# Interleaving the second batch's banded groups with buffers of their own, moving sums of v and half of the masks off PE, strided transposes with plain copies

## The chip, the cores and the metric

The kernel runs on one core of one Trainium2 chip. The time is device microseconds of the whole program on that core; the number that counts is the median of the runs. Five engines work side by side, each through its own list of instructions in a fixed order: PE (matrix products and transposes), DVE and POOL (elementwise work and reductions), ACT (elementwise functions, copies, scalings) and SP, which issues the transfers between HBM and the on-chip memory SBUF. PE writes into PSUM, eight banks of 128 partitions by 512 floats; DVE and ACT read PSUM, POOL does not.

## The reference

```python
B, H, S, D = 8, 8, 576, 64          # q, k, v: [B, H, S, D] float32, factor = 4, Sd = 144
def sm_attn(qq, kk, vv):
    s = scale * np.matmul(qq, kk.transpose(0, 1, 3, 2))
    s = s - np.max(s, axis=-1, keepdims=True)
    a = np.exp(s)
    a = a / (np.sum(a, axis=-1, keepdims=True) + 1e-09)
    return np.matmul(a, vv)
q_d = q.reshape(B, H, Sd, factor, D).mean(axis=3)     # k_d, v_d alike
out_up = np.repeat(sm_attn(q_d, k_d, v_d), factor, axis=2)
mask = np.abs(pos[:, None] - pos[None, :]) < factor
scores = np.where(mask, scale * np.matmul(q, k.transpose(0, 1, 3, 2)), -1000000000.0)
...
x = (out_up + out_local).transpose(0, 2, 1, 3).reshape(B * S, H * D)     # 4608 x 512
h = np.maximum(np.maximum(x @ w1, x @ w2), x @ w3)                       # 512 -> 768
return (h @ w_out).astype(np.float32)
```

So x is the sum of two attentions per head: one over the sequence pooled by four (144 rows, repeated four times), one local, in which a token sees itself and three neighbours on either side. On x runs a layer with three input matrices, their elementwise maximum, and one output matrix. The weights come as float64 and are decoded on the chip.

## The kernel before

Tokens of a batch are 128 pooled rows of four tokens (512) and a tail of 16 pooled rows. *Block* j (0 to 7) is the first 512 tokens of batch j; block 8 is the tails of all batches. The heads of a batch go in two *groups* of four: group n = 2j or 2j + 1.

For each block the layer (`mlp_in`, `mlp_out`) is 288 matmuls of 128x512 on PE: every product of float32 values is made as three products of split halves (`xhi` × `whi`, `xhi` × `wlo`, `xlo` × `whi`), 216 into `pm` banks for the three input matrices, and 72 for the output. Nine blocks make 2592. `transposes(j, c)` prepares block j: it adds the pooled attention `od` to the local one, then ACT rounds to `xhi` and DVE (or POOL) takes the rest as `xlo`, four tiles c of each.

The local attention is computed in two ways. Groups 4 to 15 multiply shifted windows of k and v with q and with probabilities on DVE, ACT and POOL (`scores`, `values`; names `prod`, `s`, `pv`). Groups 0 to 3 (`DENSE`) use PE, as a banded product. Their steps, by the letters that the order strings use:

- L, `band_load`: q, k, v from HBM (`q4`, `k4`, `vband` in the buffers `wo`).
- T, `band_transposes`: q and k transposed on PE into PSUM, copied into `homes` (they lie in weight buffers, so they are called `whi` and `wlo` in the trace); pairs of tokens are added on DVE into `hd` and `qkT`, the pooled q and k.
- A and B, `band_scores` for one pair of heads each: for every bank a matmul of `identr` with `maskr` puts the band's mask into PSUM, and four products of q and k are added; DVE takes the maximum (`mxb`) and ACT the exponential with its sum; POOL or ACT scales.
- V and W, `band_values`: probabilities transposed (`ptb`), copied, multiplied with `vband`, and turned into `xb` tiles of tag `x`.
- t, `tail_pooled`: the tail's rows (`traw`, `th`, `tq`). p, `pooled_scores`: scores and softmax over the 144 pooled rows (`pd`, `pdt`, `ptl`, `ptd`, `rd`), transposed on PE.
- v, `band_pooled_values`: sums of four tokens of v, as five matmuls of a constant `sums` with `vband` (four of 256 columns and one of six rows; they show as `sums` in the trace), copied to `vd`.
- o, `pooled_values`: the pooled attention's product with `vd`, scaled by ACT into `od` and, for the tail, `odtail`.

What sets the order: every operation is recorded first (`Recorder.add`), with the engines that may run it, and `place` hands them out one at a time: to the engine that could start earliest, among what is ready there by priority (`prio`, less is sooner; PE's operations get 2000 less) and then by place in the program, with durations from `price`. So an operation that two engines may run goes to where it would end sooner by these prices, and a change of a price moves work. `WINDOW` says how many PSUM tiles ahead in the program may take a free bank. The first block is written out as steps in `ORDER`, groups 0 and 1 interleaved, priority 0; group 2 has priority 200 and group 3 300, each written straight through (L T A B V t p W v o). The weights of the first four sixths come at 150 to 210, the layer at −100. Buffers are rings by tag (`prod`, `pd`, `pt`, `y`, `t`, `hqk`, ...); group 1 has a part of its own in `own1`, which lies in the buffer `prod` that group 4 needs later. One line, 374 in before and 378 in the changed kernel, emits everything, so all rows show this line.

Of the kernel before, what the change touches and what calls it, by code (L numbers as in the profile page):

```python
# [40 lines left out]
PE_MASK = (0, 1, 2, 3)  # L41
# [32 lines left out]
WINDOW = {"pa": 4, "pm": 4}  # L74
# [17 lines left out]
class Recorder:  # L92
# [44 lines left out]
    def add(self, forms):  # L137
# [18 lines left out]
        o.need, o.tiles = set(), []  # L156
# [229 lines left out]
def local_global_attention_maxout_kernel(ctx: ExitStack, tc: tile.TileContext, q, k, v, w1, w2, w3, w_out, ident_d, mask_d, diag_d, band_d, out):  # L386
# [46 lines left out]
    sums = new([P, 96 + P], tag="sums", name="sums")  # L433
# [55 lines left out]
    def load_rest():  # L489
# [4 lines left out]
        sp.dma_start(sums, band_d[:, 2 * (P + 6) :])  # L494
# [45 lines left out]
    def tail_pooled(n):  # L540
# [3 lines left out]
        for g, src in enumerate((q, k, v)):  # L544
            raw = new([N64, FAC * D], tag="traw", name=f"traw_{n}_{g}")
# [11 lines left out]
    def pooled_scores(n, tag="pa"):  # L557
# [23 lines left out]
        pd = own(n, 1).rearrange("p (a b x) -> p a b x", a=2, b=2) if n == 1 else new([P, 2, 2, SD], tag="pd", name=f"pd_{n}")  # L581
# [17 lines left out]
        pt = own(n, 2).rearrange("p (g x) -> p g x", g=HH) if n == 1 else new([P, HH, SD], tag="pt", name=f"pt_{n}")  # L599
        ptt = new([N64, P + N64], tag="hqk", bufs=2, name=f"ptt_{n}") if n == 1 else new([N64, P + N64], tag="ptt", name=f"ptt_{n}")  # L600
# [104 lines left out]
    def band_load(n):  # L705
# [10 lines left out]
        kh = st["kh"] = new([3, HH, D], tag="kd" if n == 1 else "qd", name=f"kh_{n}")  # L716
# [83 lines left out]
    def band_values(n, pr, tag):  # L800
# [7 lines left out]
        for i in range(2):  # L808
# [3 lines left out]
            pt = new([P, FAC, P], tag="t" if n == 1 else "y", bufs=2, name=f"ptb_{n}_{pr}_{i}")  # L812
# [100 lines left out]
    def attention(n):  # L913
# [3 lines left out]
        if n in DENSE:  # L917
            band_load(n)
            band_transposes(n, "pa")
            band_scores(n, 0, "pa")  # L920
            band_scores(n, 1, "pa")
            band_values(n, 0, "pa")
            tail_pooled(n)
            pooled_scores(n)
            band_values(n, 1, "pa")
            band_pooled_values(n)
            pooled_values(n)
            return
# [17 lines left out]

    def first_block():
        open_block(0)
        tags = ("pm", "pa")
        load_constants()  # L950
        for n in range(2):
            band_load(n)
        load_rest()
# [3 lines left out]
        steps = {
            "T": lambda n: band_transposes(n, tags[n]),
            "A": lambda n: band_scores(n, 0, tags[n]),
            "B": lambda n: band_scores(n, 1, tags[n]),  # L960
            "t": tail_pooled,
            "p": lambda n: pooled_scores(n, tags[n]),
            "V": lambda n: band_values(n, 0, tags[n]),
            "W": lambda n: band_values(n, 1, tags[n]),
            "v": lambda n: band_pooled_values(n, tags[n]),
            "o": lambda n: pooled_values(n, tags[n]),
        }
        for step in ORDER.split():
            steps[step[0]](int(step[1]))
# [48 lines left out]
```

## Time and profile before

| | us |
|---|---|
| median of 3 runs | 822.71 |
| lowest and highest | 818.24 and 826.49 |
| profiled execution, its time | 821.14 |
| its span in the profile | 819.4 |
| PE busy | 787.8 (96%) |
| DVE busy | 660.5 (81%) |
| ACT busy | 422.2 (52%) |
| POOL busy | 361.6 (44%) |

The span is what the profile covers; the execution's own time is 1.7 us more. All rows that follow are of this one execution, whose granted clock was 0.975 on the mean. A row of a timeline is start, length, engine, line, operation, output<-inputs by buffer names, shape and count; several like rows in line are put together, and a bracket tells idle time before and who ended it. A window's row has, for each engine, its busy time and number of instructions in that stretch, then the granted clock, the share of the DMA engines' time and GB/s.

### The profile page before, as it was taken

To read this page: it belongs to the slowest core of one execution; us is meant where nothing else is said; L and a number is where in the kernel's file an instruction comes from. 1 tells how busy PE (TensorE), PEld (TensorE's weight loads), DVE (VectorE), ACT (ScalarE), POOL (GpSimd) and SP (SyncE) were. 2 spreads that over 40 slices of the span, in tenths; PEclk is the share of its full clock that TensorE was granted. 3 is DMA by queue.
4 is the path that set the end of the run, shared out by engine and by line. 5 is a ranking of instruction groups with operands and counts; after the bars stand their busy time and mean duration, and the time that the engine had idled before them with its cause. 6 is when DMAs were issued, how large, how long until landed. Compare 5 with 4: busy or idle time off the path is not lost.

```text
span 819.4 us, 12160 instructions
## 1 busy us (share of the span) xinstructions
PE 787.8 (96%) x4064; PEld 609.9 (74%) x4064; DVE 660.5 (81%) x859; ACT 422.2 (52%) x1446; POOL 361.6 (44%) x522
## 2 busy tenths in 40 slices
PE   6879999999999999999899999999899999999997
PEld 4657776777777777777677777778677887888885
DVE  5999668799999999999999999999999962231220
ACT  7867657435583737567274746726483451121111
POOL 0642101136878847697477956768162341000000
PEclk9668999999999999999999999999999999999999
DMA  7754033334323423352234334422242210001002
GB/s 243 186 174 118 10 103 110 110 102 131 108 97 107 125 77 90 102 157 84 84 110 135 110 88 113 143 85 88 77 133 73 79 58 26 1 13 39 1 0 52
DMA packets 63177, 76.72 MB, mean 94 GB/s; under 512 B 21484, under 2 KB 43434, under 8 KB 63114
## 3 DMA queue, kind: packets, MB, share of 16 engines
q1 hardware_dynamic: 63114, 75.94, 30.8%
q8 instruction: 32, 0.52, 0.3%
q14 instruction: 31, 0.25, 0.1%
HBM read 66.49 MB, written 9.44 MB: 93 GB/s over the span
## 4 chain that ended last, share of the span: by engine, by line
PE 64%; DVE 20%; ACT 6%; issue 5%; DMA 2%; POOL 2%; POOLq 0%; SPq 0%; DVEq 0%; ACTq 0%
PE pm L374 52%; PE pa L374 11%; DVE prod L374 4%; DVE s L374 3%; DVE x L374 3%; ACT pv L374 2%; POOL pv L374 2%; DVE wo L374 1%; DMA v<-in_v_dram 1%; ACT wlo L374 1%; DVE y L374 1%; DVE pm L374 1%; DVE t L374 1%; DMA pv<-in_k_dram 1%; DVE xlo_0r L374 1%
## 5 line engine op out<-in xcount | busy, mean ns | idle before, releaser
L374 PE MATMUL pm<-xhi_0r,whi_0r 128*128 128x512 f32 x648 | 258.4, 399 | 0.0
L374 PE MATMUL pm<-xhi_0r,wlo_0r 128*128 128x512 f32 x648 | 258.3, 399 | 0.0
L374 PE MATMUL pm<-xlo_0r,whi_0r 128*128 128x512 f32 x648 | 258.2, 399 | 0.0
L374 POOL TENSOR_TENSOR pv<-v,s 128x256 f32<-128x256 f32 x247 | 177.6, 835 | 93.7 <-DVE s L374 72.1
L374 ACT ACTIVATE pv<-v,s 128x64 f32<-128x64 f32 x580 | 151.7, 412 | 21.8 <-DMA v<-in_v_dram 9.8
L374 PEld LDWEIGHTS pm<-xhi_0r,whi_0r 128*128 128x128 f32 x648 | 122.4, 189 | 28.3 <-issue 0.2
L374 PEld LDWEIGHTS pm<-xlo_0r,whi_0r 128*128 128x128 f32 x648 | 122.2, 189 | 28.1 <-issue 0.4
L374 PEld LDWEIGHTS pm<-xhi_0r,wlo_0r 128*128 128x128 f32 x648 | 122.1, 188 | 27.8
L374 DVE TENSOR_TENSOR prod<-k,q 128x1792 f32<-128x1792 f32 x56 | 119.2, 2128 | 1.1 <-DMA k<-in_k_dram 0.9
L374 DVE TENSOR_REDUCE x<-pv 128x256 f32<-128x1792 f32 x55 | 110.2, 2006 | 7.2 <-POOL pv L374 7.1
L374 DVE TENSOR_REDUCE s<-prod 128x28 f32<-128x1792 f32 x56 | 112.4, 2007 | 0.4
L374 DVE TENSOR_TENSOR t<-pm,t 128x512 f32<-128x512 f32 x54 | 36.9, 683 | 63.9 <-PE pm L374 63.8
L374 PE MATMUL pm<-wo_1r,hh_0r 128*128 128x512 f32 x216 | 85.6, 397 | 0.0
L374 PE MATMUL pm<-wo_1r,hh_1r 128*128 128x512 f32 x216 | 85.4, 399 | 0.0
L374 DVE TENSOR_TENSOR pm<-pm,t 128x512 f32<-128x512 f32 x54 | 37.3, 691 | 25.1 <-PE pm L374 24.9
L374 ACT CAST hh_1r<-pm 128x512 fp32r<-128x512 f32 x30 | 17.6, 588 | 71.3 <-DVE pm L374 71.3
L374 ACT COPY t<-pm 128x512 f32<-128x512 f32 x54 | 31.8, 589 | 40.0 <-PE pm L374 39.9
L374 ACT CAST hh_0r<-pm 128x512 fp32r<-128x512 f32 x24 | 14.1, 588 | 67.8 <-DVE pm L374 67.5
L374 PEld LDWEIGHTS pm<-wo_1r,hh_1r 128*128 128x128 f32 x216 | 41.0, 190 | 10.0 <-issue 0.5
L374 ACT COPY y<-pm 128x512 f32<-128x512 f32 x38 | 22.2, 588 | 49.6 <-PE pm L374 42.3
L374 PE MATMUL pm<-wo_0r,hh_1r 128*128 128x512 f32 x120 | 47.5, 400 | 0.1
L374 PEld LDWEIGHTS pm<-wo_1r,hh_0r 128*128 128x128 f32 x216 | 40.9, 189 | 9.1
(262 smaller groups left out, 1142.6 us busy)
## 6 DMA issues: line engine op xcount, KB each, us to landing
v<-in_v_dram SPq DMA_DIRECT2D x55, 320.0 KB
k<-in_k_dram SPq DMA_DIRECT2D x55, 320.0 KB
out_dram<-y SPq DMA_DIRECT2D x36, 256.0 KB
q<-in_q_dram SPq DMA_DIRECT2D x56, 128.0 KB
hh<-in_moe_w_dram SPq DMA_DIRECT2D x12, 512.0 KB
pv<-in_moe_w_dram SPq DMA_DIRECT2D x6, 512.0 KB
pv<-in_moe_w_out_dram SPq DMA_DIRECT2D x6, 512.0 KB
wo<-in_v_dram SPq DMA_DIRECT2D x12, 128.0 KB
```

What stands on the lines that cost most here:

```text
L374: getattr(self.engines[o.eng], method)(*map(real, args), **{k: real(x) for k, x in kw.items()})
```

## The change

Six edits:

1. Group 3 gets buffers of its own as group 1 has them (`OTHER`): its `qkT`, `pd` and `pt` in `own1`, `kh` in `kd`, `ptt` in `hqk`. Only group 1 keeps its `ptb` in `t` (`TY`).
2. Groups 2 and 3 are written in steps, interleaved (`ORDER2`, `second_block`), both at priority 200.
3. In groups 2 and 3 the mask is added by DVE, from PSUM into SBUF, and the maximum and the exponential read it there; the identity matmuls stay in groups 0 and 1 alone (`PE_MASK`).
4. `band_pooled_values` no longer uses PE: v is loaded again, 128 KB for each head, and halved twice by additions on DVE or POOL. The constant `sums` goes.
5. In groups 0 and 1 the transposes of q and k write PSUM in the tokens' order, every fourth word, and the copies out of PSUM become plain; before, the transposes wrote plainly and the copies were strided on both sides.
6. The order's parameters: `WINDOW` from 4 to 3, POOL's price of `tensor_scalar` from 2.2 to 4.1 ns for each element, `traw` of k and v in groups 0 and 1 in the ring `q`. `GATE` and `behind` have empty values and do nothing.

```diff
+OTHER = (1, 3)
+TY = (1,)
+ORDER2 = "L2 T2 L3 A2 B2 V2 W2 T3 t2 p2 A3 B3 v2 o2 V3 W3 t3 p3 v3 o3"
 ORDER = "T0 T1 A0 A1 B0 V0 B1 V1 t0 p0 t1 p1 W0 W1 v0 o0 v1 o1"
-PE_MASK = (0, 1, 2, 3)
+PE_MASK = (0, 1)
-WINDOW = {"pa": 4, "pm": 4}
+WINDOW = {"pa": 3, "pm": 3}
...
             if method == "tensor_copy":
                 return 180.0 + n, True
+            if method == "tensor_scalar":
+                return 140.0 + 4.1 * n, True
...
         sp.dma_start(diag, diag_d)
-        sp.dma_start(sums, band_d[:, 2 * (P + 6) :])
         sp.dma_start(mask, mask_d.rearrange("m p x -> p m x"))
...
         for g, src in enumerate((q, k, v)):
-            raw = new([N64, FAC * D], tag="traw", name=f"traw_{n}_{g}")
+            raw = new([N64, FAC * D], tag="q", bufs=2, name=f"traw_{n}_{g}") if n < 2 and g else new([N64, FAC * D], tag="traw", name=f"traw_{n}_{g}")
...
-        pd = own(n, 1).rearrange("p (a b x) -> p a b x", a=2, b=2) if n == 1 else new([P, 2, 2, SD], tag="pd", name=f"pd_{n}")
+        pd = own(n, 1).rearrange("p (a b x) -> p a b x", a=2, b=2) if n in OTHER else new([P, 2, 2, SD], tag="pd", name=f"pd_{n}")
...
+                    inorder = ps.rearrange("p (r f) -> p f r", f=FAC)
                     for f in range(FAC):
-                        pe.transpose(ps[:, P * f : P * f + P], byf[:, f], ident)
-                    to, fr = dst.rearrange("p (r f) -> p f r", f=FAC), ps.rearrange("p (f r) -> p f r", f=FAC)
+                        pe.transpose(inorder[:, f], byf[:, f], ident)
+                    to, fr = dst, ps
...
-        banks = {}
+        banks, on_pe = {}, n in PE_MASK
...
-            for i in range(2):
+            for i in range(2) if on_pe else ():
                 pe.matmul(sps[i], identr, rest, start=True, stop=False, skip_group_check=True)
-                banks[tp, i] = sps[i]
...
-                    pe.matmul(sps[i][:, u], qT[pp, t0 : t0 + P], kT[pp, t0 : t0 + P + 6], start=False, stop=u == 1, skip_group_check=True)
+                    pe.matmul(sps[i][:, u], qT[pp, t0 : t0 + P], kT[pp, t0 : t0 + P + 6], start=not on_pe, stop=not on_pe or u == 1, skip_group_check=True)
+            for i in range(2):
+                banks[tp, i] = sps[i]
+                if not on_pe:
+                    dve.tensor_tensor(out=sm[:, i, 2 * tp : 2 * tp + 2], in0=sps[i], in1=rest.bitcast(F32), op=ALU.add)
+                    banks[tp, i] = sm[:, i, 2 * tp : 2 * tp + 2]
...
-            pt = new([P, FAC, P], tag="t" if n == 1 else "y", bufs=2, name=f"ptb_{n}_{pr}_{i}")
+            pt = new([P, FAC, P], tag="t" if n in TY else "y", bufs=2, name=f"ptb_{n}_{pr}_{i}")
...
-    def band_pooled_values(n, tag="pa"):
+    def band_pooled_values(n):
         j, h0 = n // 2, HH * (n % 2)
-        st = state[n]
-        vt, vb = st["vband"], st["vb"]
-        vd = st["vd"] = new([P, HH, D], tag="vd", bufs=2, name=f"vd_{n}")
-        ps = bank([P, HH, D], tag, f"psv_{n}")
-        for u in range(FAC):
-            pe.matmul(ps, sums[:, 96 - 32 * u : 96 - 32 * u + P], vt[:, u], start=u == 0, stop=False, skip_group_check=True)
-        pe.matmul(ps[96:], sums[:6, 64:96], vb[1][:, 1], start=False, stop=True, tile_position=(0, 96), skip_group_check=True)
-        copy(vd, ps)
+        hv = new([P, HH, 2 * D], tag="hv", name=f"hv_{n}")
+        vd = state[n]["vd"] = new([P, HH, D], tag="vd", bufs=2, name=f"vd_{n}")
+        for g in range(HH):
+            vv = new([P, FAC * D], tag="v", bufs=2, name=f"v_{n}_{g}")
+            sp.dma_start(vv, row_tokens(v, j, h0 + g, 0, FAC * D))
+            halves(n, "v", vv, hv[:, g], BENG)
+        tt(vd, hv[:, :, :D], hv[:, :, D:], ALU.add, BENG)
...
+    def second_block():
+        open_block(1)
+        if 3 in DENSE:
+            steps_of(ORDER2, ("pa", "pa"))
...
-    block(1)
+    with at(200.0, LAG):
+        second_block()
```

How the instructions move. On PE, around the transposes of group 3's pooled probabilities; `pd_507` and `pdt_530` are group 3's probabilities in before, `y_349,wo_229` and `wlo_0_324,k_94` its W step, `sums_133` its sums of v, rows with `512` the layer's matmuls. Before:

```order
L374 MATMUL pm_126<-xhi_0r,whi_0r 128x512
L374 MATMUL pa_176<-ident_65,pd_507 128x128 x4
L374 MATMUL pa_157<-ident_65,pdt_530 128x64
L374 MATMUL pa_157<-ident_65,ptl_548 64x128
L374 MATMUL pa_157<-ident_65,ptd_553 64x64
L374 MATMUL pa_166<-ident_65,wlo_0_324 128x128 x4
L374 MATMUL pa_149<-y_349,wo_229 64x128
L374 MATMUL pa_176<-wo_229,sums_133 128x256 x4
L374 MATMUL pa_176<-k_97,sums_133 32x256
L374 MATMUL pa_149<-y_382,wo_229 64x128
L374 MATMUL pa_149<-y_349,wo_229 64x128
```

In the changed kernel, where the probabilities are `prod_207` and `pdt_547`:

```order
L378 MATMUL pm_129<-xhi_0r,whi_0r 128x512
L378 MATMUL pm_129<-xhi_0r,wlo_0r 128x512
L378 MATMUL pa_173<-ident_65,pdt_547 128x64
L378 MATMUL pa_173<-ident_65,ptl_575 64x128
L378 MATMUL pa_155<-ident_65,prod_207 128x128 x4
L378 MATMUL pa_173<-ident_65,ptd_593 64x64
L378 MATMUL pa_185<-ident_65,tq_222 128x64 x2
L378 MATMUL pm_129<-xlo_0r,whi_0r 128x512
L378 MATMUL pm_129<-xhi_0r,whi_0r 128x512
L378 MATMUL pm_129<-xhi_0r,wlo_0r 128x512
L378 MATMUL pm_129<-xlo_0r,whi_0r 128x512
```

The W step of group 3 and its sums no longer stand behind the transposes: the former is ahead, the latter is gone, and more of the layer's matmuls are ahead (173 against 147).

On DVE, around the addition of `od` to group 2's local attention (`x_...<-x_...,od_...`). `hd` and `qkT` are group 3's pooled q and k, `zd`, `rd`, `ptl` and `pd` group 2's pooled softmax, `zb` group 3's local one, `wo_...` the decoding of weights, `y` copies of transposed probabilities, `hh` and `t` the layer's. Before:

```order
L374 TENSOR_TENSOR hh_0r<-pm_126,hh_1r 128x512
L374 TENSOR_SCALAR zd_71<-zd_71 128x5
L374 RECIPROCAL rd_545<-zd_71 128x5
L374 TENSOR_TENSOR ptl_548<-pd_507,rd_545 128x2x2x16
L374 TENSOR_TENSOR pd_507<-pd_507,rd_545 128x4x128
L374 TENSOR_TENSOR t_470<-pm_104,t_470 128x512
L374 TENSOR_TENSOR x_1020<-x_1020,od_1146 128x512
L374 TENSOR_TENSOR x_454<-x_454,od_1146 128x512
L374 TENSOR_TENSOR hd_144<-whi_0_73 128x256
L374 TENSOR_TENSOR qkT_146<-hd_144 128x128
```

After:

```order
L378 TENSOR_SCALAR zb_286<-zb_286 128x4
L378 RECIPROCAL zb_286<-zb_286 128x4
L378 TENSOR_SCALAR wo_257<-wo_257 128x512
L378 COPY y_377<-pa_173 128x512
L378 TENSOR_SCALAR zb_286<-zb_286 128x4
L378 RECIPROCAL zb_286<-zb_286 128x4
L378 SCALAR_TENSOR_TENSOR wo_257<-pv_81,wo_257 128x512
L378 TENSOR_TENSOR x_1052<-x_1052,od_1372 128x512
L378 TENSOR_TENSOR x_467<-x_467,od_1372 128x512
L378 TENSOR_TENSOR wlo_0r<-wo_257,whi_0r 128x512
```

Group 3's pooled pairs stood behind the addition; in the changed kernel they are well ahead of it, group 3's local softmax (`zb`) stands just ahead, and weight operations among it.

On SP, in the first transfers; `q_109` is the mask of the band, `hh` the weights and group 1's q and k, `traw` the tails, `pv` group 2's q. Before:

```order
L374 DMA q_109<-in_band_dram 128x268
L374 DMA diag_123<-in_diag_dram 64x4
L374 DMA sums_133<-in_band_dram 128x224
L374 DMA mask_155<-in_mask_dram 128x2x12
L374 DMA traw_171<-in_q_dram 64x1x256
L374 DMA hh_174<-in_moe_w_dram 128x4x256 x3
L374 DMA hh_87<-in_moe_w_dram 128x4x256 x3
L374 DMA traw_171<-in_k_dram 64x1x256
L374 DMA pv_81<-in_q_dram 128x4x64
```

After, with the first two loads of v for the new additions (`v_171`, `v_183`):

```order
L378 DMA q_109<-in_band_dram 128x268
L378 DMA diag_120<-in_diag_dram 64x4
L378 DMA mask_131<-in_mask_dram 128x2x12
L378 DMA traw_153<-in_q_dram 64x1x256
L378 DMA q_166<-in_k_dram 64x1x256
L378 DMA v_171<-in_v_dram 128x256
L378 DMA v_183<-in_v_dram 128x256
L378 DMA q_109<-in_v_dram 64x1x256
L378 DMA hh_197<-in_moe_w_dram 128x4x256 x2
L378 DMA traw_153<-in_q_dram 64x1x256
L378 DMA hh_197<-in_moe_w_dram 128x4x256
L378 DMA hh_87<-in_moe_w_dram 128x4x256 x3
```

`sums` is gone, and the tails of k and v and two loads of v are ahead of the weights.

More of the change, by code (lines that the diff above doesn't have):

```diff
@@ L32 @@
 XBUFS = 5
+OTHER = (1, 3)
+TY = (1,)
+ORDER2 = "L2 T2 L3 A2 B2 V2 W2 T3 t2 p2 A3 B3 v2 o2 V3 W3 t3 p3 v3 o3"
+GATE = ("", "", "", "")
 QENG = ("DVE",)
@@ L62, in shape_constants @@
     band = np.stack([np.where(np.arange(P + 6) < 3, np.float32(-8.0e9), band), band], 1)
-    c = np.arange(P)[:, None] - 3 - 4 * (np.arange(96 + P)[None, :] - 96)
-    sums = ((c >= 0) & (c < FAC)).astype(np.float32)
-    band = np.concatenate([band.reshape(P, -1), sums], axis=1)
+    band = band.reshape(P, -1)
     return ident, mask, diag, np.ascontiguousarray(band.astype(np.float32))
@@ L102, in __init__ @@
         self.ops, self.tags, self.of, self.masks = [], {}, {}, {}
-        self.prio, self.lag = 0.0, 0.0
+        self.prio, self.lag, self.behind = 0.0, 0.0, set()
         self.engines = {"PE": nc.tensor, "DVE": nc.vector, "ACT": nc.scalar, "POOL": nc.gpsimd, "SP": nc.sync}
@@ L155, in add @@
         o.seq = len(self.ops)
-        o.need, o.tiles = set(), []
+        o.need, o.tiles = set() if "SP" in forms else set(self.behind), []
         pe = "PE" in forms
@@ L432, in local_global_attention_maxout_kernel @@
     KW = SEG + 6
-    sums = new([P, 96 + P], tag="sums", name="sums")
     KB = 2 * FAC * (P + 6)
@@ L598, in pooled_scores @@
         act.mul(pdt[:, :P], pdt[:, :P], rd[:N64, 4:5])
-        pt = own(n, 2).rearrange("p (g x) -> p g x", g=HH) if n == 1 else new([P, HH, SD], tag="pt", name=f"pt_{n}")
-        ptt = new([N64, P + N64], tag="hqk", bufs=2, name=f"ptt_{n}") if n == 1 else new([N64, P + N64], tag="ptt", name=f"ptt_{n}")
+        pt = own(n, 2).rearrange("p (g x) -> p g x", g=HH) if n in OTHER else new([P, HH, SD], tag="pt", name=f"pt_{n}")
+        ptt = new([N64, P + N64], tag="hqk", bufs=2, name=f"ptt_{n}") if n in OTHER else new([N64, P + N64], tag="ptt", name=f"ptt_{n}")
         pst1 = bank([P, HH, P], tag, f"pt1_{n}")
@@ L715, in band_load @@
         st["q4"], st["k4"] = q4, k4
-        kh = st["kh"] = new([3, HH, D], tag="kd" if n == 1 else "qd", name=f"kh_{n}")
+        kh = st["kh"] = new([3, HH, D], tag="kd" if n in OTHER else "qd", name=f"kh_{n}")
         base = (j * H + h0) * S * D
@@ L737, in band_transposes @@
         q4, k4, kh = st["q4"], st["k4"], st["kh"]
-        qkT = st["qkT"] = own(n, 0).rearrange("p (a b x) -> p a b x", a=2, b=2) if n == 1 else new([P, 2, 2, SD], tag="qkT", name=f"qkT_{n}")
+        qkT = st["qkT"] = own(n, 0).rearrange("p (a b x) -> p a b x", a=2, b=2) if n in OTHER else new([P, 2, 2, SD], tag="qkT", name=f"qkT_{n}")
         for pr in range(2):
@@ L916, in attention @@
             open_block(j)
[L917 to L928, printed above, removed]
         scores(n)
@@ L945, in turn, with steps_of @@
                 transposes(j, c)
+    mark = {}
+    def steps_of(order, tags):
+        steps = {
+            "L": band_load,
+            "T": lambda n: band_transposes(n, tags[n % 2]),
+            "A": lambda n: band_scores(n, 0, tags[n % 2]),
+            "B": lambda n: band_scores(n, 1, tags[n % 2]),
+            "t": tail_pooled,
+            "p": lambda n: pooled_scores(n, tags[n % 2]),
+            "V": lambda n: band_values(n, 0, tags[n % 2]),
+            "W": lambda n: band_values(n, 1, tags[n % 2]),
+            "v": band_pooled_values,
+            "o": lambda n: pooled_values(n, tags[n % 2]),
+        }
+        for step in order.split():
+            steps[step[0]](int(step[1]))
+            mark[step] = rec.ops[-1]
     def first_block():
         open_block(0)
-        tags = ("pm", "pa")
         load_constants()
-        for n in range(2):
-            band_load(n)
+        steps_of("L0 L1", ("pm", "pa"))
         load_rest()
@@ L956, in first_block @@
                 keep_busy(WARM, "warm0")
[L957 to L969, printed above, removed]
+        steps_of(ORDER, ("pm", "pa"))
+    def second_block():
+        open_block(1)
+        if 3 in DENSE:
+            steps_of(ORDER2, ("pa", "pa"))
+        else:
+            steps_of("L2 T2 A2 B2 V2 t2 p2 W2 v2 o2", ("pa", "pa"))
+            attention(3)
     with at(0.0, LAG):
@@ L973, in local_global_attention_maxout_kernel @@
     for ft in range(NFT - 2):
+        rec.behind = {mark[GATE[ft]]} if GATE[ft] else set()
         with at(W0 + WSTEP * ft):
             weight_in(ft)
+    rec.behind = set()
     turn(0)
-    block(1)
+    with at(200.0, LAG):
+        second_block()
     for ft in range(NFT - 2, NFT):
```

## The prediction

> **What bounds the kernel now.** I read the page's busy times, its forty slices, the chain of waits, PE's waits, then windows and timelines of the first 150 us, where all of the change lies.
>
> ```profile
> PE 787.8 (96%) x4064; PEld 609.9 (74%) x4064; DVE 660.5 (81%) x859; ACT 422.2 (52%) x1446; POOL 361.6 (44%) x522
> ...
> PE   6879999999999999999899999999899999999997
> ...
> DVE  5999668799999999999999999999999962231220
> ...
> PEclk9668999999999999999999999999999999999999
> ...
> 680.92 132.73 PE pm L374 x571
> ...
> PE pa L374 <- DVE ptl L374: 2.2, 1, 2.2
> ...
> PE pm L374 <- DVE vd L374: 0.9, 1, 0.9
> ```
>
> PE is busy 96% of 819.4 us; its only thin slices are the first three (the granted clock also drops there, to 0.6). The last piece of the chain is 571 MLP matmuls in 132.73 us, 0.2325 us for each (start to start; the 0.40 us of a single row overlaps its neighbours). Of PE's waits, the 2.2 us on `ptl` come near 391 us, far behind the change, and the 0.9 us on `vd` are PE waiting for the copy of group 0's sums. So from the first MLP matmul on, time goes only when PE gets fewer instructions or when its holes close. The second engine is DVE, nearly full to 660 us except in two or three slices near 100 us:
>
> ```profile
> 10.00:20.00 10.00, 8.85 (x72) 6.85 (x70) 8.18 (x25) 9.78 (x26) 0.45 (x1) 1.00 0.77 248
> 20.00:80.00 60.00, 51.70 (x389) 37.07 (x390) 57.09 (x133) 44.31 (x161) 26.69 (x20) 0.74 0.63 166
> 80.00:120.00 40.00, 40.00 (x280) 29.83 (x278) 26.01 (x62) 22.45 (x78) 3.89 (x5) 1.00 0.18 53
> 120.00:141.40 21.40, 20.05 (x138) 14.71 (x137) 20.34 (x47) 17.05 (x63) 3.07 (x4) 1.00 0.35 114
> ```
>
> DVE's busy time is the third figure: 8.18 of 10, 57.09 of 60, 26.01 of 40, 20.34 of 21.4. It idles 1.8 + 2.9 + 14.0 + 1.1 = 19.8 us between 10 and 141.4, and 14.0 of that while group 2's banded work waits for PE and ACT. The clock is 0.74 in 20 to 80 and 1.00 afterwards.
>
> **The place by which I measure.** The transposes of group 3's pooled probabilities are the last PE work of the second batch that needs DVE.
>
> ```profile
> 49.44 3.28 PE L374 MATMUL pm<-wo,sums 128*128 128x256 f32 x8
> 52.65 0.76 PE L374 MATMUL pa<-prod 64*128 64x144 f32 x8
> ...
> 56.20 0.61 PE L374 MATMUL pm<-wo,sums 6*32 6x256 f32 x2
> ...
> 63.58 3.04 PE L374 MATMUL pa<-wo,sums 128*128 128x256 f32 x8
> ...
> 67.10 1.09 PE L374 MATMUL pa<-t,wo 128*64 128x128 f32 x14
> ...
> 73.08 0.39 PE L374 MATMUL pm<-xhi_0r,whi_0r 128*128 128x512 f32 x1
> ...
> 142.43 0.60 PE L374 MATMUL pa<-ident,pd 128*128 128x128 f32 x4
> ...
> 143.57 0.66 PE L374 MATMUL pa<-ident,wlo 128*128 128x128 f32 x4
> ...
> 144.52 1.99 PE L374 MATMUL pa<-wo,sums 128*128 128x256 f32 x8
> ...
> 146.99 1.09 PE L374 MATMUL pa<-y,wo 128*64 128x128 f32 x14
> ...
> 148.57 0.47 PE L374 MATMUL pa<-pt,vd 128*64 128x144 f32 x4
> ```
>
> In before they start at 142.43, with 147 MLP matmuls ahead; in the new order 173 stand ahead, and group 3's W step (143.57 to 148.57 without its sums, 5.0 − 2.5 = 2.5 us) as well. At the old pace PE would be there at 142.43 + 26 × 0.2325 + 2.5 = 151.0.
>
> **Sums of v leave PE.** Each group's 20 matmuls go: 146.99 − 144.52 = 2.5 us for group 3, and I take 2.5 for group 2; 3.2 + 0.6 us (49.44 to 52.65 and the row at 56.20) for group 0, 3.5 us (63.58 to 67.10) for group 1. I count all of it as in line, since PE had little else to run there. Instead 16 v tiles are loaded again and halved.
>
> **Masks.** Groups 2 and 3 lose 16 identity matmuls.
>
> ```profile
> 75.75 0.50 PE L374 MATMUL pm<-xhi_0r,whi_0r 128*128 128x512 f32 x1
> 76.09 0.40 PE L374 MATMUL pm<-xhi_0r,wlo_0r 128*128 128x512 f32 x1
> ...
> 109.30 0.29 PE L374 MATMUL pa<-maskr_0r,identr_0r 128*128 128x268 f32 x1
> 109.42 0.39 PE L374 MATMUL pm<-xlo_0r,whi_0r 128*128 128x512 f32 x1
> ...
> 113.30 0.39 PE L374 MATMUL pa<-maskr_0r,identr_0r 128*128 128x268 f32 x1
> 113.62 0.72 PE L374 MATMUL pa<-wlo 64*128 64x134 f32 x4
> ```
>
> A mask costs PE between 109.42 − 109.30 = 0.12 and 113.62 − 113.30 = 0.32 us; at the middle, 0.22, 16 make 3.5 us. The first MLP matmul after other work takes 0.34 (75.75 to 76.09) instead of 0.2325, 0.11 more. The new order has 16 fewer such switches in all; counting half of them here, 0.9. Together 4.4 us.
>
> **The first MLP matmul.** Two engines could hold it back. PE: 73.08 − 7.3 of sums − 0.9 of waiting for their copy = 64.9. DVE, which makes the `xlo` tiles:
>
> ```profile
> 69.34 1.89 DVE L374 TENSOR_TENSOR wlo_0r<-wo,whi_0r 128x512 fp32r<-128x512 f32 x3
> ...
> 98.57 0.69 DVE L374 TENSOR_TENSOR t<-pm,t 128x512 f32<-128x512 f32 x1 [2.42 <-PE pm L374]
> 107.03 1.29 DVE L374 TENSOR_TENSOR x<-x,od 128x512 f32<-128x512 f32 x2 [7.77 <-ACT od L374]
> ...
> 140.73 0.68 DVE L374 TENSOR_TENSOR pd<-pd,rd 128x512 f32<-128x512 f32 x1
> ...
> L374 DVE TENSOR_REDUCE mxb<-pa 128x2 f32<-128x268 f32 x24 | 9.4, 426 | 0.3 <-ACT whi L374 0.3
> ...
> L374 DVE TENSOR_TENSOR qkT<-hd 128x128 f32<-128x128 f32 x12 | 3.5, 293 | 0.4
> ...
> L374 DVE TENSOR_TENSOR hv<-v 128x128 f32<-128x128 f32 x14 | 14.8, 1071 | 0.2
> ...
> L374 POOL TENSOR_SCALAR wo<-wo 128x512 f32<-128x512 f32 x7 | 15.6, 2237 | 20.3 <-ACT wo L374 20.3
> ```
>
> A 128x512 DVE operation costs 0.60 to 0.68 us (the first row: three in 1.89; the last: one in 0.68). By such prices DVE has 3.5 us less to do ahead of the second `xlo` tile, since three pooled scalings, copies and weight operations went elsewhere or later: 69.34 − 3.5 = 65.8. I take 66.5, so 6.5 us earlier than 73.08.
>
> **DVE's added work up to that place.** 16 mask additions of 128x268; before shows none. The reduction of the same width, 0.426 us alone and about 0.35 start to start, is the nearest row: 5.6 us (bounds: 0.21, the short addition's pace, and 0.60, the 128x512 one's: 3.4 to 9.6). 12 of the 16 halvings of v at 0.21: 2.5 us; the row for just this operation says 1.07 us when POOL is at work too, an upper bound of 12.8. Additions that finish v: 1.0. Six weight clamps leave POOL, 2.24 us each there, for DVE at about 0.34: 2.0. Two plain copies 1.2. Gone: 4.2 (three scalings, two copies, the tails' small sums). Lasting 8.1 us. Besides, 8.6 us of weight and MLP operations that stood later now stand ahead of the place (some 15, between 0.3 and 0.65 each). Together 16.7.
>
> DVE's last operation ahead of the place ends at 141.3 in before (140.73 and 0.6). The interleaving lets group 3's work fill the holes, such as 7.77 us of waiting for `od` at 107.03 and 2.42 us at 98.57. Of 19.8 us I leave 6 idle (what waits for loads at the start, 1.8, and some 4 for PE's and ACT's answers), so 13.8 are used: 141.3 + 16.7 − 13.8 = 144.2.
>
> **PE's side of the place.** 151.0 − 6.5 (start) − 2.5 (group 2's sums) − 4.4 (masks) − 1.3 (idle in 120 to 141.4: 20.05 busy of 21.4) = 136.3, say 137.
>
> PE thus waits for DVE, until 144.2 and 0.3 for the handing over: 144.5. Gain 151.0 − 144.5 = 6.5, and group 3's sums, behind the place, 2.5: 9.0. Of the 2.2 us on `ptl` near 391 half may vanish with the earlier work; I count 1.1. Sum 10.1: 821.1 − 10.1 = 811.0 for the profiled execution, which ran 1.6 us under the median of 822.7; I make no difference of that.
>
> **What I cost at nothing.** The strided PSUM writes let seven copies in the first 20 us go plain:
>
> ```profile
> 8.71 1.16 ACT L374 ACTIVATE wlo<-pm 128x512 f32<-128x512 f32 x1
> ...
> 71.93 0.58 ACT L374 COPY whi<-pa 128x512 f32<-128x512 f32 x1
> ...
> 37.54 0.90 SPq L374 DMA_DIRECT2D v<-in_v_dram  x2
> ```
>
> 0.6 us less each on ACT, whose 9.78 busy us of 10 to 20 make that part of the start, but DVE and the loads hold it as well (PE's row at 64.9 is ahead of DVE's 65.8), so it is inside my 66.5. Sixteen loads of 128 KB take 0.45 us each of SP's queue (the last row: two in 0.90). Two of them stand ahead of all weights: about 1 us, hidden, since the weights are first multiplied after 60; uncovered it is the same 1 us at the first MLP matmul. The third to eighth stand among the weights and the second batch's loads, and wait there for a halving of v on DVE or POOL that frees one of two buffers; whatever is behind them on SP waits too. DMA is 0.77 busy in 10 to 20 and 0.18 in 80 to 120, so what is late can catch up; I count nothing, at worst the few us of C. The PSUM window of 3 and POOL's dearer price only change the order, which is counted. Behind the place DVE has 16.7 − 13.8 = 2.9 us of delay and 8.6 of work done early; the next blocks' tiles are no later.
>
> **Rivals.** *B, DVE's holes take everything.* If 14 or more us are filled and DVE's additions come at their lower bounds (3.4 + 2.5), PE alone sets the place: 151.0 − 137 + 2.5 + 1.1 = 17.6 less, 803.5. For it: 19.8 us idle; against: the idle time left must fall to about zero, and each of the four windows shows some.
>
> *C, the expected gain is lost on DVE: the same.* The halvings at 1.07 instead of 0.21 add 10.3 us, or the interleaved chains leave 14 us idle rather than 6: 8 to 10 us later at the place, 819 to 821. For it: the row of 1.07 us, and the 2.2 to 2.4 us waits that a new order may put elsewhere.
>
> *D, slower: strided transposes.* The change writes 32 transposes of the first batch to every fourth word of PSUM, all in the start's chain.
>
> ```profile
> 6.35 1.97 PE L374 MATMUL pm<-ident,xhi 128*128 128x128 f32 x8 [6.35 <-DVE xhi L374]
> ```
>
> Eight take 1.97 us here, about 0.24 each. Twice as long, they would add 32 × 0.24 = 7.6 us, of which 5 in line: 816; at four times, 23 us, some 20 in line: 831. It ends on the other side of 821 from about three times. The nearest row is ACT's copy, 1.16 us strided against 0.58 plain, a factor of 2, and on another engine. [...]
>
> **Chances.** Forecast 0.50 (own range 806 to 816, from halvings and masks at their bounds and idle time between 2 and 11); B 0.16; C 0.24; D 0.10, of which about half stays near 816. The range from 804 to 823 leaves out the lower half of B and the upper half of D. Within 1% (8.2 us, about what a measurement of this kernel can tell from no change, given runs from 818 to 826): most of C (0.20), the top of the forecast (0.09) and the mild D (0.04) make 0.33; the rest of the forecast and B, faster, 0.57; the rest of C and D, slower, 0.10.
>
> **What would show it.** The first MLP matmul at 66.5 (C and D: 70 and later); no sums rows, and mask rows for groups 0 and 1 alone; DVE idle about 6 us in 10 to 145 rather than 19.8; a wait of PE for DVE of several us ahead of group 3's pooled transposes, near 137 to 144 (B: none); transposes in the first 12 us at 0.24 each (D: 0.5 or more); halvings of v on DVE near 0.25 (C: 1). I am wrong if PE's wait is longer than about 8 us there, if later blocks' `xlo` tiles become late, or if the start is no earlier.

## The result and the profile after

The changed kernel takes 812.79 us (median of 4 runs, 812.62 to 813.46) against 822.39 us before (818.24 to 826.49): a ratio of 0.9888, 95% interval 0.9861 to 0.9914, so 1.1% faster. The forecast was 811.0 in a range of 804 to 823. The profiled execution has a span of 811.1 us, 8.3 us less.

The busy times and slices of the changed kernel:

```profile
PE 780.5 (96%) x4008; PEld 606.9 (75%) x4008; DVE 660.3 (81%) x885; ACT 423.5 (52%) x1456; POOL 350.5 (43%) x525
...
PE   6989999998999999999999998999999999999997
...
DVE  5799989999999999999999999999999851231220
...
PEclk9558999999999999999999999999999999999999
```

PE has 7 us less work and DVE as much as before, but DVE's hole near 100 us (the slices 6, 6, 8 in before, 9, 8, 9 now) is shut. The same windows as before, the last one a little longer:

```profile
10.00:20.00 10.00, 8.51 (x67) 6.56 (x65) 8.88 (x26) 3.92 (x18) 2.89 (x7) 1.00 0.64 187
20.00:80.00 60.00, 55.44 (x376) 40.09 (x377) 52.93 (x137) 46.45 (x167) 12.28 (x13) 0.66 0.69 187
80.00:120.00 40.00, 39.46 (x278) 29.75 (x278) 36.69 (x97) 29.98 (x106) 7.62 (x10) 1.00 0.32 104
120.00:145.00 25.00, 23.81 (x174) 17.34 (x172) 24.34 (x53) 18.22 (x55) 4.17 (x6) 1.00 0.43 136
```

DVE idles 1.1 + 7.1 + 3.3 + 0.7 = 12.2 us where it idled 19.8, and the clock granted to PE is 0.66 in 20 to 80, where it was 0.74. The two for which PE waits longest behind the start (total, times, longest):

```profile
PE pa L378 <- DVE ptl L378: 5.3, 2, 3.7
PE pa L378 <- DVE xlo_0r L378: 4.3, 2, 3.2
```

The rows of PE's timeline that answer to the prediction's, and the two longest of these waits:

```profile
5.57 1.97 PE L378 MATMUL pm<-ident,xhi 128*128 128x128 f32 x8 [5.57 <-DVE xhi L378]
7.33 1.91 PE L378 MATMUL pm<-ident,xlo 128*128 128x128 f32 x8
...
71.26 0.50 PE L378 MATMUL pm<-xhi_0r,whi_0r 128*128 128x512 f32 x1
...
144.95 0.27 PE L378 MATMUL pa<-ident,pdt 64*128 64x64 f32 x1 [0.92 <-ACT pdt L378]
...
202.36 0.30 PE L378 MATMUL pa<-ident,ptl 128*64 128x128 f32 x1 [3.67 <-DVE ptl L378]
...
492.18 0.33 PE L378 MATMUL pa<-ident,tq 64*128 64x64 f32 x2 [3.24 <-DVE xlo_0r L378]
```

Eight strided transposes take 1.97 us. The first layer matmul is at 71.26 (73.08 before, 66.5 forecast). Group 3's pooled transposes start at 144.95 (144.5 forecast, 151.0 at the old pace), after a wait of 0.92 us that ACT ends, with `pdt`. At 202.36 and 492.18 PE then waits 3.67 and 3.24 us for DVE, in blocks that the change does not touch.

### The profile page after: what moved, and what is told of

Same layout as the page of the kernel before. It is cut to its first block, busy times and chain, and to the rows that moved or that the text cites. A ratio compares the mean times of both kernels' runs of the same rounds, so it can differ in the third digit from the quotient of the medians.

```text
span 811.1 us, 12109 instructions
## 1 busy us (share of the span) xinstructions
PE 780.5 (96%) x4008; PEld 606.9 (75%) x4008; DVE 660.3 (81%) x885; ACT 423.5 (52%) x1456; POOL 350.5 (43%) x525
## 4 chain that ended last, share of the span: by engine, by line
PE 70%; DVE 19%; ACT 4%; issue 3%; DMA 2%; SPq 1%; DVEq 0%; ACTq 0%
PE pm L378 59%; PE pa L378 11%; DVE s L378 3%; DVE prod L378 3%; DVE x L378 2%; ACT pv L378 2%; DVE y L378 2%; DMA hh<-in_moe_w_dram 1%; DVE wo L378 1%; DVE xlo_0r L378 1%; DVE ptl L378 1%; DMA hh<-in_k_dram 1%; DVE pm L378 1%; DVE t L378 1%; ACT pd L378 1%
## 5 line engine op out<-in xcount | busy, mean ns | idle before, releaser
L378 POOL TENSOR_TENSOR pv<-v,s 128x256 f32<-128x256 f32 x250 | 182.6, 848 | 80.3 <-DVE s L378 65.9
L378 ACT ACTIVATE pv<-v,s 128x64 f32<-128x64 f32 x568 | 148.0, 410 | 27.8 <-DMA v<-in_v_dram 8.2
L378 PEld LDWEIGHTS pm<-wo_1r,hh_1r 128*128 128x128 f32 x216 | 40.9, 189 | 10.4 <-issue 0.5
L378 POOL TENSOR_TENSOR hqk<-q 128x128 f32<-128x128 f32 x47 | 25.6, 544 | 52.5 <-DMA q<-in_q_dram 52.4
```

The costliest lines, as they stand in the source:

```text
L378: getattr(self.engines[o.eng], method)(*map(real, args), **{k: real(x) for k, x in kw.items()})
```

## The experiments

Each kernel is the changed one with the edit shown, unless it says otherwise. The ratio is to the kernel before on the same chip. To compare where the time is, I take from each profiled execution the starts of PE's matmuls: the *first* layer matmul; the *stalls* behind it, gaps from one start to the next of more than 1.0 us, less 0.23 us; the time at *half* clock behind it; and the *rest*, which is the time from the first layer matmul to the last, less the stalls and less half of the time at half clock. The rest stands for PE's work. All four are of the one profiled execution, and the half clock is that of the record of granted clocks. At half clock a layer matmul took 0.43 us from start to start (203.35 to 203.78 in the changed kernel), at the full clock 0.23 (206.25 to 206.48), 0.20 less: that the price of this time is half of it is my estimate from these two.

| kernel | median us | ratio, 95% interval | first | stalls | half | rest |
|---|---|---|---|---|---|---|
| before | 822.39 | 1 | 73.1 | 6.1 | 6.8 | 730.7 |
| changed | 812.79 | 0.9888 (0.9861 to 0.9914) | 71.3 | 12.4 | 6.8 | 717.9 |
| e1_sums01 | 818.30 | 0.9956 (0.9926 to 0.9985) | 69.3 | 11.2 | 23.9 | 719.7 |
| e2_sums23 | 826.98 | 1.0060 (1.0026 to 1.0095) | 68.4 | 15.9 | 25.4 | 722.5 |
| e3_masks | 812.82 | 0.9877 (0.9830 to 0.9924) | 69.7 | 8.2 | 10.2 | 721.6 |
| e4_plain | 815.21 | 0.9914 (0.9886 to 0.9942) | 74.1 | 14.0 | 16.0 | 717.3 |
| e5_straight | 829.28 | 1.0107 (1.0066 to 1.0148) | 69.4 | 22.8 | 23.9 | 717.7 |
| e6_params | 818.51 | 0.9985 (0.9954 to 1.0016) | 70.1 | 9.4 | 20.5 | 721.7 |
| e7_warm40 | 821.30 | 1.0009 (0.9985 to 1.0033) | 74.6 | 12.7 | 26.8 | 716.4 |
| e8_warm100 | 834.02 | 1.0175 (1.0134 to 1.0217) | 69.5 | 22.6 | 23.9 | 725.6 |
| e9_interleave_alone | 830.22 | 1.0094 (1.0064 to 1.0125) | 74.3 | 14.2 | 17.1 | 724.5 |
| e10_lag1200 | 822.68 | 1.0009 (0.9987 to 1.0030) | 80.9 | 6.3 | 17.1 | 719.9 |
| e11_lag2000 | 850.43 | 1.0365 (1.0301 to 1.0429) | 86.4 | 21.2 | 41.0 | 714.5 |
| e12_late1200 | 802.32 | 0.9779 (0.9750 to 0.9809) | 70.2 | 6.9 | 0 | 716.8 |

In e1, 30 matmuls of attention that stand ahead of the first layer matmul in the changed kernel stand behind it, and in e8 33 of the added matmuls do, so their first and rest are not those of the others. The runs e1 to e8, e9 to e11 and e12 are of three chips; differences in us below are between medians, and by the ratios some come out otherwise (e6 8.0 us instead of 5.7, e12 9.0 instead of 10.5). One execution is a sample: in e4 it took 821.4, 6 us more than its median.

**Sums of groups 0 and 1 back on PE** (with the constant `sums` and its load).

```diff
...
+        if n in (0, 1):
+            for u in range(FAC):
+                pe.matmul(ps, sums[:, 96 - 32 * u : 96 - 32 * u + P], vt[:, u], start=u == 0, stop=False, skip_group_check=True)
+            pe.matmul(ps[96:], sums[:6, 64:96], vb[1][:, 1], start=False, stop=True, tile_position=(0, 96), skip_group_check=True)
+            copy(vd, ps)
+            return
```

> The changed kernel with the sums of v of groups 0 and 1 on PE again (20 matmuls each), all else as changed. In the changed kernel's trace PE's clock is half from 22 to 42 and from about 46 to 66 us, 41 us in all, against 31 before, and the first matmul of the layer is only 1.8 us earlier. Theory A (what the start gained by losing these sums was given back by the lower clock): 0 to 2.5 us slower than the changed kernel, 813 to 815.5, with less time at half clock than 41 us. Rival B (the start's gain of 6.5 us is there and something else ate it): about 6 us slower, 819.

It took 5.5 us more than the changed kernel, nearer to B by the time. Its trace does not bear B out, though: the first layer matmul is at 69.3, earlier and not later, with all the sums ahead of it:

```profile
57.85 2.44 PE L380 MATMUL pa<-wo,sums 128*128 128x256 f32 x10
...
64.11 1.99 PE L380 MATMUL pa<-wo,sums 128*128 128x256 f32 x8
66.04 0.61 PE L380 MATMUL pa<-k,sums 6*32 6x256 f32 x2
...
69.30 0.50 PE L380 MATMUL pm<-xhi_0r,whi_0r 128*128 128x512 f32 x1 [1.62 <-ACT xhi_0r L380]
```

Here they run at the full clock (1.00 granted) and take 2.4 and 2.5 us (57.85 to 60.22, 64.11 to 66.58), 4.8 in all, where the prediction read 7.3 in before. What the run loses is 17 us more at half clock behind the first layer matmul (71.7 to 81.9, and in three stretches later), 8.5 us. So neither theory had it: the 41 us of low clock up to 82 came, but partly behind the first layer matmul.

**Sums of groups 2 and 3 back on PE** (the same edit with `(2, 3)`).

> The changed kernel with the sums of v of groups 2 and 3 on PE again. These run while PE is full. Theory A (PE sets the pace from the first layer matmul on): two times 2.47 us more, 817.8. Rival C (DVE sets the pace at the transposes of group 3's pooled probabilities, as the prediction had it): the sums of group 2 hide in PE's wait there and DVE gets lighter, so at most 2.5 us more, 815 or less.

14.2 us slower. The rest grew by 4.6 us, close to A's 5.0, and nothing was hidden as C had it. The other 10 us are stalls (+3.5) and half clock (+18.6, so 9.3 us), less an earlier start (−2.8): more than A said, in terms that it did not contain.

**Masks of groups 2 and 3 back on PE.**

```diff
-PE_MASK = (0, 1)
+PE_MASK = (0, 1, 2, 3)
```

> The changed kernel with the masks of groups 2 and 3 added by identity matmuls on PE again. Theory A (PE sets the pace): 16 times 0.22 us, 3.5, and up to 0.9 for switches: 816.3 to 817.2. Rival C (DVE sets the pace): 5.6 us less on DVE, so no slower than 813 or even faster.

The same time, 812.8. The rest grew by 3.7 us, which is A's price, and the stalls fell by 4.2, which fits C (the start is 1.6 us earlier, and half clock costs 1.7 more): what PE saves by the masks comes back as waits. That DVE's additions make these waits is the likely reading, not a shown one, since the order moved with them.

**Plain transposes, strided copies again.**

```diff
-                        pe.transpose(inorder[:, f], byf[:, f], ident)
-                    to, fr = dst, ps
+                        pe.transpose(ps[:, P * f : P * f + P], byf[:, f], ident)
+                    to, fr = dst.rearrange("p (r f) -> p f r", f=FAC), ps.rearrange("p (f r) -> p f r", f=FAC)
```

> The changed kernel with plain transposes and strided copies in groups 0 and 1 as before; the order of the instructions stays. Theory A (a strided write costs PE nothing, since eight transposes take 1.97 us either way in the two traces; a strided copy costs ACT and DVE 0.6 us more, seven of them in the first 20 us, partly in line): 0.5 to 2.5 us slower, 813.3 to 815.3. Rival D (strided writes do cost PE): faster than the changed kernel.

2.4 us slower, in A's range, though its interval overlaps the changed kernel's. The mechanism is read from rows. PE's transposes when they write plainly:

```profile
5.63 1.97 PE L378 MATMUL pm<-ident,xhi 128*128 128x128 f32 x8 [5.63 <-DVE xhi L378]
7.39 1.91 PE L378 MATMUL pm<-ident,xlo 128*128 128x128 f32 x8
```

ACT's copy of the first tile out of PSUM in the same kernel, strided:

```profile
7.26 1.08 ACT L378 ACTIVATE whi<-pm 128x512 f32<-128x512 f32 x1
```

and in the changed kernel, plain:

```profile
7.12 0.59 ACT L378 ACTIVATE whi<-pm 128x512 f32<-128x512 f32 x1
```

PE's eight transposes take 1.97 and 1.91 us either way; the copy falls from 1.08 to 0.59. Rival D is out.

**Groups 2 and 3 straight through again.**

```diff
-OTHER = (1, 3)
+OTHER = (1,)
...
-            steps_of(ORDER2, ("pa", "pa"))
+            steps_of("L2 T2 A2 B2 V2 t2 p2 W2 v2 o2", ("pa", "pa"))
+            with at(300.0, LAG):
+                steps_of("L3 T3 A3 B3 V3 t3 p3 W3 v3 o3", ("pa", "pa"))
```

> The changed kernel with groups 2 and 3 written straight through again, at priorities 200 and 300, and group 3 without buffers of its own; sums, masks, transposes and parameters as changed. Theory A (the gain is PE work that is gone, and stalls and the clock decide the rest): PE's work after the first layer matmul stays within 2 us of the changed kernel's, and the time is 811 to 817 by its stalls. Rival C (the interleaving makes the gain by filling DVE's idle time): 817 to 822.

16.5 us slower than the changed kernel, 1.1% slower than before. The rest is the same (717.7), as A said, but its range for the time was far too low: stalls rose by 10.4 us and half clock by 17. A window of this kernel:

```profile
120.00:145.00 25.00, 20.17 (x109) 14.29 (x108) 20.32 (x54) 19.73 (x71) 3.80 (x4) 0.73 0.33 108
```

and two of PE's waits:

```profile
PE pm L378 <- ACT wo_1r L378: 5.8, 2, 4.3
...
PE pa L378 <- ACT y L378: 3.6, 1, 3.6
```

DVE is busy 20.32 of 25 us where the changed kernel has 24.34; over 10 to 145 it idles 135 − 114.7 = 20.3 us, about as before the change (22.0 over the same stretch). So without the interleaving DVE's holes stay, and PE waits for copies and for the output weights (`wo_1r`). That these are late because of DVE's added work, so that the interleaving is what makes room for the rest, is the likely reading; this run does not show it.

**The order's parameters back.**

```diff
-WINDOW = {"pa": 3, "pm": 3}
+WINDOW = {"pa": 4, "pm": 4}
...
-                return 140.0 + 4.1 * n, True
+                return 140.0 + 2.2 * n, True
```

> The changed kernel with the order's two parameters as before (a PSUM window of 4, POOL's scalar operations priced 2.2 ns for each element). Theory A: PE's work the same or up to 2 us more (15 more switches between the layer and other work, 0.11 us each), the rest by its stalls: 811 to 818. Rival: the parameters carry most of the gain, 819 to 822.

5.7 us slower, just above A's range. The rest is 3.9 us higher with 15 more changes between the layer and other work (95 against 80 in the order); if it is all theirs, 0.26 us for each instead of the 0.11 that I had. Half clock costs 6.8 us more. Stalls and the start are 4.2 us less.

**Matmuls to keep PE busy at the start.**

```diff
-WARM = 0
+WARM = 40
```

> The changed kernel with 40 matmuls of 128x512 on the identity added, whose result nobody reads, in places of the first batch where PE has nothing else ready (20 ahead of the first transposes, 20 between the first scores and the first products). Theory A (PE's idle time there lets the clock fall to half, and the low clock holds the start back): less than 41 us at half clock in the first 80, and the first layer matmul 2 to 5 us earlier than 71.2: 808 to 812. Rival B (the low clock comes anyway, and the added matmuls stand in line): 813 to 820.

8.5 us slower, on B's side and beyond its range. The clock was better in 20 to 80 (0.78 against 0.66), but the first layer matmul came 3.4 us later, and 20 us more at half clock behind it cost 10.0. With 100 of them:

> As the run before with 100 such matmuls, 40 of the further ones later in the first batch, among transposes and scores of the pooled rows. Theory A: less than 20 us at half clock, the first layer matmul 3 to 6 us earlier, 806 to 812. Rival B: in line with 0.23 to 0.43 us each, 8 to 17 us later for 40 of them: 820 to 830.

834.02 us, beyond both ranges: the stalls are 22.6 us, and 33 of the added matmuls stand behind the first layer matmul (the rest is 7.7 higher). Its windows show what is left when the clock is nearly full:

```profile
20.00:80.00 60.00, 52.15 (x420) 38.45 (x420) 58.94 (x135) 44.10 (x150) 14.91 (x18) 0.94 0.70 191
```

The clock is 0.94 and DVE busy 58.94 of 60 us, and the first layer matmul is at 69.5, less than 2 us earlier. So the low clock is not the only thing that holds the start; DVE is near its limit there. How much of it the clock alone would give could not be told apart, since the added matmuls also stand in line and move other work in the order.

**The interleaving alone, on the kernel before** (sums and masks on PE, plain transposes, the old parameters; group 3's buffers and the ring of the first tails as changed).

> The kernel before with the interleaving of groups 2 and 3 and their buffers alone (and the ring of the first tails): sums and all masks on PE, plain transposes, the old parameters. If the parts add up, the interleaving's 16.5 us (measured by undoing it) come out here too: near 806. Theory A (PE's work and its stalls): PE's work after the first layer matmul is 9 to 13 us above the changed kernel's, so that it can be no faster than the kernel before by more than its stalls (6 us and their time at half clock): 816 to 826. Rival C (the interleaving makes the gain): 812 or less.

830.2 us, 0.9% slower than before and beyond A's range. The parts do not add up: undoing the interleaving costs 16.5 us, doing it alone costs 8. The rest (724.5) lies 6.6 above the changed kernel's, below A's 9 to 13; eight stalls make 14.2 us.

**Later readiness in the planning of the order.**

```diff
-LAG = 600.0
+LAG = 1200.0
```

> The changed kernel with one number changed: in the order's planning, an operation of attention that needs another engine's result is taken to be ready 1200 ns after it instead of 600. Nothing is computed otherwise; PE's list then has the layer's matmuls where it had attention's early transposes (group 4's pooled transposes stand behind 416 layer matmuls instead of 370). Theory A (the changed kernel loses 12.4 us in PE's stalls from the first layer matmul on, and 3.5 us in the half clock that follows two of them, because its list puts attention's transposes ahead of when DVE is ready): stalls fall below 8 us, time 805 to 811. Rival (the stalls only move, as DVE is the bound in the middle): 811 to 818.

The stalls fell to 6.3 us, as A said, but the first layer matmul came 10 us later, as the first batch was planned with the longer time too, and half clock cost 5 us more: 822.7, beyond both ranges. With 2000:

> As the run before with 2000 ns. Theory A: stalls below 6 us unless the attention comes so late that a block's tiles are awaited: 803 to 811. Rival: 811 to 820.

850.43 us: the first layer matmul at 86.4, 21.2 us of stalls of which 7.5 at the place of group 3's pooled transposes. Both ranges that I gave were wrong. The last one leaves the first two batches alone:

```diff
+LATE = 1200.0
...
-            with at(100.0 * n, LAG):
+            with at(100.0 * n, LATE):
...
-        with at(-200.0, LAG):
+        with at(-200.0, LATE if j > 1 else LAG):
```

> The changed kernel with the 1200 ns only from block 2 on; PE's list stays as it is up to group 3's pooled transposes (173 layer matmuls ahead of them), and group 4's stand behind 405 instead of 370. In the run with 1200 ns everywhere the stalls from the first layer matmul on fell from 12.4 to 6.3 us, but the first layer matmul came 10 us later. Theory A (the start and the stalls behind block 1 are separate terms): the first layer matmul within 3 us of 71.2, the 3.8 us stall at 202 gone, 806 to 811. Rival (the stalls come from DVE being late and only move): 812 to 818.

802.32 us, faster than A's range; its interval (0.9750 to 0.9809) lies wholly below the changed kernel's (0.9861 to 0.9914): a version that beats both. The page of this kernel:

```profile
span 800.1 us, 12116 instructions
...
PE 771.2 (96%) x4008; PEld 600.6 (75%) x4008; DVE 648.7 (81%) x891; ACT 425.2 (53%) x1463; POOL 367.5 (46%) x526
...
PE   5879999999999999999999999999999999999997
...
PEclk9758999999999999999999999999999999999999
```

Against the changed kernel its profiled execution gains 11.0 us of span: 5.5 in stalls (the longest left is 1.6 us), 3.4 in half clock (none is left behind the start until the output at the end), 1.0 at the start, 1.1 in the rest.

## Why the prediction was right, step by step

The time and its sign were right, 1.8 us off. By the terms above the gain of 8.3 us of span is 1.8 at the start and 12.8 in PE's work, less 6.3 in added stalls. The forecast had 10.1: too much for the start (6.5) and for the stalls (1.1 less instead of 6.3 more), too little for PE's work (9.4 by its terms: 2.5 + 4.4 + 2.5). So it is partly luck that the number is this close.

**The first layer matmul, forecast 66.5, measured 71.26: wrong.** The step that failed is PE's side, "73.08 − 7.3 of sums − 0.9". DVE's side held: the second `xlo` tile was forecast for 65.8 and was ready at 66.8 (65.52 and 1.29). PE has then still 4.5 us of attention ahead of the layer, at almost the full clock:

```profile
65.52 1.29 DVE L378 TENSOR_TENSOR xlo_0r<-x,xhi_0r 128x512 fp32r<-128x512 f32 x2
...
66.00:71.00 5.00, 5.00 (x60) 4.02 (x60) 4.26 (x10) 4.42 (x11) 2.25 (x1) 0.98 0.34 76
```

Two windows of the start, before first and changed second:

```profile
21.00:66.00 45.00, 37.01 (x268) 26.21 (x269) 42.64 (x100) 33.42 (x123) 22.11 (x14) 0.66 0.64 174
```

```profile
21.00:66.00 45.00, 41.44 (x261) 29.33 (x262) 39.01 (x101) 36.54 (x140) 8.69 (x9) 0.55 0.71 198
```

PE is busy longer (41.44 against 37.01 of 45 us) at a lower clock (0.55 against 0.66). The 7.3 us of sums were a price at a low clock, as their rows showed (3.28 us with 0.59 granted from 49.44 to 52.65, and 3.04 with 0.69 from 63.58 to 67.10, for what took group 3 only 1.99 at 1.00; 4.8 for both groups in e1, at 1.00), and I took them as if the clock would not change. With them gone, the clock was at half for 41 us ahead of the first layer matmul instead of 31. It is tempting to put the lost 5 us down to that. But e12, e3 and e5 have the same 408 matmuls in the same order ahead of their first layer matmul as the changed kernel. The windows up to it, in the order changed, e12, e3, e5:

```profile
0.00:71.26 71.26, 59.64 (x409) 44.19 (x409) 55.33 (x150) 51.47 (x178) 14.70 (x21) 0.71 0.68 195
```

```profile
0.00:70.21 70.21, 54.08 (x409) 40.17 (x409) 55.61 (x150) 51.64 (x178) 14.13 (x21) 0.76 0.69 198
```

```profile
0.00:69.69 69.69, 59.21 (x409) 43.85 (x410) 55.45 (x151) 51.46 (x178) 12.53 (x20) 0.68 0.69 199
```

```profile
0.00:69.39 69.39, 58.71 (x408) 43.33 (x409) 54.85 (x149) 50.97 (x178) 13.30 (x21) 0.68 0.69 200
```

With 34 us at half clock against 41, e12 has PE busy for 5.6 us less but idle for 16.1 us instead of 11.6, and comes only 1.0 us earlier; e3 and e5, with 44 us at half clock, come earlier still. So a better clock is in part only waited away, and this list of PE gives 69.4 to 71.3 with 34 to 44 us at half clock (e4 has the same list behind slower copies: 74.1, with 52). So PE's side is not had by taking the removed durations off 73.08; how much of the loss is the clock's and how much is waiting for other engines stays open. (A group's sums are 10 rows of the trace, not 20 matmuls as the prediction has it; its price was read from the rows and does not depend on the count.)

**PE's arrival at group 3's pooled transposes, forecast 137, measured 144.0; DVE's, forecast 144.2, measured 144.5.** Rows of DVE's timeline, two of them ahead of the place (three mask additions, two halvings), two at it, and ACT's operation behind them for which PE waits:

```profile
76.75 1.11 DVE L378 TENSOR_TENSOR whi<-pa,maskr_0r 128x268 f32<-128x268 f32 x3
...
85.21 0.48 DVE L378 TENSOR_TENSOR hv<-v 128x128 f32<-128x128 f32 x2
...
144.04 0.18 DVE L378 RECIPROCAL rd<-zd 128x5 f32<-128x5 f32 x1
...
144.31 0.21 DVE L378 TENSOR_TENSOR ptl<-prod,rd 128x64 f32<-128x64 f32 x1
...
144.51 0.38 ACT L378 ACTIVATE pdt<-pdt,rd 64x128 f32<-64x128 f32 x1
```

The mask additions cost 1.11 / 3 = 0.37 us each (0.35 forecast), halvings 0.24 (0.21). The single prices held, but the sum of 16.7 us did not: DVE was busy 122.8 us from 10 to 145 and 111.6 from 10 to 141.4 before, 11.2 more, and idle for 12.2 instead of 6. Two errors of about 6 us cancel in its 144.5. The place itself (144.95 against 144.5) then came out right with a wait of PE of 0.9 us instead of 7, because PE came 7 us late, 4.8 of them from the start. That is a right number by offsets, so luck. A bound of DVE at this place, the forecast's mechanism, is not shown: the several us of PE's wait that were to be its sign did not come, and it is B's sign ("B: none") that is nearer.

**Sums and masks of groups 2 and 3: right in size.** 5.0 and 3.5 us forecast, 4.6 and 3.7 by e2 and e3. The extra 0.9 us for switches is open: e6 speaks for 0.26 us each, e9, with as many changes as e6, for less. PE's whole work fell by 12.8 us. Sums, masks and parameters, undone one at a time, make 4.6 + 3.7 + 3.9 = 12.2 of it, but e9 has 6.2 less than before without any of the three, so these do not simply add.

**Stalls behind the second batch: wrong.** I counted a gain of 1.1 near 391. That stall is gone, but others came at 202 and 492, 3.84 and 3.41 us by their gaps, where PE's list has transposes ahead of DVE's results. "The next blocks' tiles are no later" was true, but a transpose may stall where no block's tile is late. e12 shows their price and that they are matters of order.

**What I cost at nothing.** The strided transposes: right, nothing on PE (1.97 us for eight, strided and plain). The plain copies, 0.5 us less each, were inside the 66.5; e4 gives 2.4 us for both, hardly clear of the noise. The order's parameters: wrong, 5.7 us by e6.

**The rivals.** B (803.5, DVE's holes take everything) did not come: the start missed, and DVE stayed idle for 12.2 us. C's price for the halvings (1.07 us) did not come either. D is refuted.

## What to carry to other kernels

Where an engine's list is fixed ahead of time, price a change in two parts: the work that it removes from the bounding engine, which came out here within 0.4 us for sums and masks undone alone, and the stalls that its new order makes, which moved by 10 us for the same work between two orders. Before undoing or adding parts, look where the bounding engine now stalls, in stretches that the change does not touch: one number there was worth about as much as the whole change. A duration that was read at a low clock was not what its removal gave: the sums of groups 0 and 1 were read at 7.3 us, 0.6 of it at the full clock and the rest with 0.59 and 0.69 granted; they took 4.8 at 1.00 in e1, and without them the first layer matmul came 1.8 earlier.

## What the runs showed of the hardware

Two short stalls of PE cost more than themselves in the changed kernel. After the wait of 3.67 us that ended at 202.36, the granted clock was 0.53 from 202.5 to 206, though PE was busy throughout, and it was 0.51 from 492.8 to 496.3, behind the wait of 3.24; behind the one of 1.66 us that ended at 446.56 it stayed full (1.00 from 446.5 to 450). In e12, without the two long stalls, it was never half behind the start until the last output (1.00 throughout, from 70.5 to 800). But a full PE was not enough to get the clock back, nor always to keep it: the last of these rows is of before, where it fell to 0.50 from 151.1 to 154.5 without any gap of more than 1 us from 73.1 on.

```profile
28.00:32.00 4.00, 4.00 (x27) 3.31 (x26) 1.50 (x5) 1.72 (x10) 2.16 (x2) 0.50 0.40 91
32.00:36.00 4.00, 4.00 (x22) 2.10 (x21) 3.09 (x9) 3.95 (x23) 1.96 (x2) 0.50 0.67 151
36.00:40.00 4.00, 4.00 (x44) 3.10 (x46) 3.32 (x10) 3.19 (x8) 0.21 (x1) 0.50 0.87 221
202.50:206.00 3.50, 3.50 (x10) 2.68 (x10) 3.50 (x4) 1.98 (x9) 2.39 (x1) 0.53 0.50 132
```

```profile
148.00:156.00 8.00, 8.00 (x54) 6.17 (x54) 7.29 (x13) 3.72 (x11) 1.36 (x2) 0.79 0.46 150
```

In the changed kernel PE is busy 4.00 of 4.00 us in three windows with the attention's small matmuls, and the clock is 0.50 in all three; with the layer's matmuls it came back after 3.5 us (0.53 from 202.5 to 206, 0.98 from 206 to 209). What tells these 12 us at half clock from the 3.5, and what made the clock fall in before at 151.1 with PE busy, was not tried.

Strided PSUM writes: eight transposes of 128x128 float32 that write every fourth word took 1.97 us in the changed kernel, 0.24 each, and eight plain ones took 1.97 in e4 as well.
